# Lightning attention into an MLP: groups of one chunk of each sequence, and eight first MLP blocks on three chunks

## The chip, the cores and the metric

The kernel runs on one core of a Trainium2 chip. The core has five engines, each with its own instruction stream: TensorE (PE; its weight loads are listed as PEld), VectorE (DVE), ScalarE (ACT), GpSimd (POOL) and SyncE (SP). They run side by side and wait for each other through semaphores; transfers run on 16 DMA engines. The metric is the time of one execution on the device in microseconds, the median over runs; lower is better. Every instruction stream keeps the order in which the program emits it: the scheduling is manual, so the order of the Python calls is the order on each engine.

## The reference

Four sequences of 768 positions, eight heads of 64. Linear attention with a decay per head goes over a sequence in blocks, carrying a 64 x 64 state per head; its output is the input of an MLP with an exact GELU.

```python
for b in range(nb):
    intra = np.einsum('bhic,bhjc->bhij', qb, kb) * Dmask[None]
    intra = np.einsum('bhij,bhjd->bhid', intra, vb)
    inter = np.einsum('bhid,bhde->bhie', qb * lam_pow[None], kv_state)
    out[:, :, sl] = intra + inter
    kb_dec = kb * rev_pow[None]
    kv_state = lam_block[None, :, None, None] * kv_state + np.einsum('bhsd,bhse->bhde', kb_dec, vb)
x = out.transpose(0, 2, 1, 3).reshape(B * S, H * D)     # 3072 x 512
h = x @ w_in                                            # 512 -> 2048
g = 0.5 * h * (1.0 + erf(h / sqrt(2)))
return g @ w_out                                        # 2048 -> 512
```

Inputs and output are float32; matrix products take bfloat16 operands, into which the loads convert.

## The kernel before

The kernel uses chunks of 128 positions, so each of the four sequences has six, 24 in all. Chunk n is sequence n // 6, position n % 6: chunks 0 to 5 are the first sequence in order. Four consecutive chunks form a group, of 512 token rows, and the MLP runs on a group at a time; there are six groups.

A chunk passes through these steps. `load` (line 64) issues a transfer of q, k or v from GpSimd's queue. `decay_v` (146) multiplies v by a decay into `v_dec`, on VectorE for the first two chunks and on GpSimd for all others. `transposes` (151) turns k and q on TensorE, and ScalarE copies kT out while VectorE scales qT (chunks 0 to 7); chunks from 8 on are turned by DMA instead, issued from SyncE's queue (`dma_transposes`, 167). `scores` (173) multiplies kT and qT on TensorE, and VectorE masks the two halves into `sc_m`. `next_state` (184) multiplies k and `v_dec` on TensorE, and VectorE adds the previous state and scales the sum; it is left out for the last chunk of a sequence. `outputs` (227) multiplies state and qT (unless the chunk is the first of its sequence), adds `v_dec` times `sc_m`, and copies the sum into x, on ScalarE for chunks 0 to 7 and VectorE afterwards. State and output of the first four chunks use a special form with half-filled 64 x 64 matmuls (lines 189 to 210 and 233 to 238).

`mlp_blocks` (406) gives a group as a list of blocks. Sixteen `mm1` blocks multiply w_in with x, four matmuls of 512 columns each, and ScalarE applies GELU. Then group 0 has 16 `mm2` blocks of four matmuls of 512 columns against w_out. Groups 1 to 5 have 14 blocks that form the same product from seven half-sized products (`blocks_by_seven`, 275), with sums of g and of w_out made by VectorE between them (`g_sum`, `w_out_sum`); the products `m1` and `m7` share a bank `r`, and a VectorE step at line 386 (`f_x`) reads it between them.

The lead-in (lines 477 to 511) runs chunks 0 to 3 up to x, with idle matmuls (`keep_warm`) in between, before any MLP block. While the MLP of group g runs, the chunks of group g + 1 are prepared: for group 0 the dictionary `group0` (539) says which steps run ahead of which block; for later groups `todo` (552) places them by the share of matmul columns done. Loads go through GpSimd's queue in the order of the program, with `decay_v` in the same queue; a load also waits until the eighth transfer before it has landed (as its waits in the trace show). w_in comes in four pieces of 512 columns (512 KB each), the first after the loads of chunks 0 to 3, the fourth behind `decay_v` of chunk 3, then w_out in four.

Of the kernel before, what the change touches and what calls it, by code (L numbers as in the profile page):

```python
# [15 lines left out]
def kernel(  # L16
# [25 lines left out]
    assert NG * M == NCH and M == 4 and NB == 6  # L42
# [13 lines left out]

    raw = {}
    dram = dict(q=q, k=k, v=v)

    def chunk_of(name, n):  # L60
        b, so = n // NB, n % NB
        return dram[name][b, :, so * C:(so + 1) * C, :].rearrange("h si d -> si h d")
# [14 lines left out]
    for item in "k0 q0 v0 k1 q1 k2 q2 v1 k3 q3 v2 v3".split():  # L77
        load(int(item[1]), item[0])
# [7 lines left out]
    def load_w_in(s):  # L86
        f = d_ff // NS
        nc.gpsimd.dma_start(w_in_t[:, :, s * f:(s + 1) * f], w_in_r[:, :, s * f:(s + 1) * f])
# [16 lines left out]
    first_blk = consts.tile([128, HP, 128], BF16)  # L105
    nc.vector.memset(lam_blk, 0.0)
    nc.vector.memset(first_blk, 0.0)
# [32 lines left out]
    def begin(n, early=False):  # L140
        c = Chunk()
        c.n, c.sb, c.early = n, n % NB, early
        c.q, c.k, c.v = (raw.pop((n, name)) for name in "qkv")
        return c

    def decay_v(c, eng):

        c.v_dec = work_pool.tile([128, H, D], BF16, tag="vd", name="v_dec")
        eng.tensor_mul(c.v_dec, c.v, lam_m[:, :, None].to_broadcast((128, H, D)))  # L149

    def transposes(c, between=lambda: None):

        t_ps = [bank([128, HP, C], BF16, tag, "t_ps") for tag in ("mh", "mo" if c.early else "mh")]
        for dst, src in zip(t_ps, (c.k, c.q)):
            for hp in range(HP):
                nc.tensor.transpose(dst[:, hp, :], src[:, 2 * hp:2 * hp + 2, :], ident)  # L156
            if src is c.k:
                between()
        c.kT = work_pool.tile([128, HP, C], BF16, tag="kT", name="kT")
        c.qT = work_pool.tile([128, HP, C], BF16, tag="qT", name="qT")  # L160
        if c.n > 0:
# [22 lines left out]
    def next_state(c):  # L184
        if c.sb == NB - 1:
            return
        if not c.early:
            return next_state_full(c)
        kv_ps = bank([128, HP, D], F32, "t", "kv_ps")
        for hp in range(HP):  # L190
            for hi in range(2):
                h = 2 * hp + hi
                nc.tensor.matmul(kv_ps[hi * D:(hi + 1) * D, hp, :], c.k[:, h, :], c.v_dec[:, h, :],
                                 start=True, stop=True)
        if c.n == M - 1:
            tmp = work_pool.tile([128, HP, D], F32, tag="tmp", name="tmp")
            nc.vector.tensor_add(tmp, kv_ps, states[c.n][0])
            for hi in range(2):
                p = slice(hi * D, (hi + 1) * D)
                nc.vector.tensor_mul(first_blk[p, :, p], tmp[p], lam_c_b[p])  # L200
            states[c.n + 1] = first_blk, None
            return
        new = work_pool.tile([128, HP, D], BF16, tag="state", name="state")
        if c.sb == 0:
            nc.vector.tensor_mul(new, kv_ps, lam_c_b)
        else:
            tmp = work_pool.tile([128, HP, D], F32, tag="tmp", name="tmp")
            nc.vector.tensor_add(tmp, kv_ps, states[c.n][0])
            nc.vector.tensor_mul(new, tmp, lam_c_b)
        states[c.n + 1] = new, None  # L210

    def next_state_full(c):

        kv_ps = bank([128, HP, 128], F32, "t", "kv_ps")
        for hp in range(HP):
            nc.tensor.matmul(kv_ps[:, hp, :], c.k[:, 2 * hp:2 * hp + 2, :], c.v_dec[:, 2 * hp:2 * hp + 2, :],
                             start=True, stop=True)
        new = work_pool.tile([128, HP, 128], BF16, tag="state_f", name="state")
        if c.sb == 0:
            nc.vector.tensor_mul(new, kv_ps, lam_blk)  # L220
        else:
            tmp = work_pool.tile([128, HP, 128], F32, tag="tmp", name="tmp")
            nc.vector.tensor_add(tmp, kv_ps, states[c.n][0])
            nc.vector.tensor_mul(new, tmp, lam_blk)  # L224
        states[c.n + 1] = new, None

    def outputs(c, x_t, off, evacuate=True):
        o_ps = bank([128, HP, C], F32, "o", "o_ps")
        if c.sb > 0 and not c.early:
            for hp in range(HP):  # L230
                nc.tensor.matmul(o_ps[:, hp, :], states[c.n][0][:, hp, :], c.qT[:, hp, :],  # L231
                                 start=(hp == 0), stop=False, skip_group_check=True)
        elif c.sb > 0:
            for hp in range(HP):
                for hi in range(2):
                    p = slice(hi * D, (hi + 1) * D)
                    nc.tensor.matmul(o_ps[p, hp, :], states[c.n][0][p, hp, :], c.qT[p, hp, :],
                                     start=(hp == 0), stop=False, skip_group_check=True)
        for hp in range(HP):
            for hi in range(2):  # L240
                nc.tensor.matmul(o_ps[hi * D:(hi + 1) * D, hp, :], c.v_dec[:, 2 * hp + hi, :], c.sc_m[:, hp, hi, :],  # L241
                                 start=(c.sb == 0 and hp == 0), stop=True, skip_group_check=True)
# [32 lines left out]
    def blocks_by_seven(g, g_t, first):  # L275
# [47 lines left out]
        def store(rows, us, cols):  # L323
            r = g * M * C + rows * 2 * C
            dst = out[r + us.start * C:r + us.stop * C, cols].rearrange("(u p) d -> p u d", p=C)
            nc.sync.dma_start(dst, sb["o0" if rows == 0 else "o1"][:, us, cols])
# [78 lines left out]

    def mlp_blocks(g):
# [4 lines left out]
        def mm1(kf):  # L411
            def run():
                h_ps = bank([128, T], F32, "mh", "h_ps")

                parts = [(0, T - C), (T - C, T)] if g == 0 and kf == 0 else [(0, T)]
                for lo, hi in parts:
                    for ki in range(NK1):
                        nc.tensor.matmul(h_ps[:, lo:hi], w_in_t[:, ki, kf * 128:(kf + 1) * 128], x_t[:, ki, lo:hi],  # L418
                                         start=(ki == 0 and lo == 0), stop=(ki == NK1 - 1), skip_group_check=True)
                nc.scalar.activation(g_t[:, kf, :], h_ps, ACT.Gelu)  # L420
# [4 lines left out]
        def mm2(io, part):  # L425
            def run():
# [5 lines left out]
                if part == NK2 // 4 - 1:  # L432
                    o_sb = out_pool.tile([128, d_model], F32, tag="o_s", name="o_sb")
                    r = (g * M + io) * C
                    nc.scalar.copy(o_sb, om[io])
                    nc.sync.dma_start(out[r:r + C, :], o_sb)
# [3 lines left out]
        blocks = [(mm1(kf), 4 * T) for kf in range(NK2)]  # L440
        if g > 0:
            return blocks_by_seven(g, g_t, blocks)
# [58 lines left out]
    empty_outputs(live[1])
    next_state(live[2])
    outputs(live[2], xT[0], 2)
    scores(live[3])
    keep_warm(4)
    outputs(live[3], xT[0], 3)
    make_lam_blk()
    load_w_in(3)
# [8 lines left out]
    for n, name in [(4, "k"), (4, "q"), (4, "v"), (5, "k"), (5, "q"), (5, "v"), (6, "k"), (6, "q")]:  # L517
        load(n, name)
    begin_decayed(4)
    for n, name in [(6, "v"), (7, "k"), (7, "q"), (7, "v"), (8, "k")]:  # L520
        load(n, name)
    begin_decayed(5)
    begin_decayed(6)
    for n, name in [(8, "q"), (8, "v")]:
        load(n, name)
    begin_decayed(7)
    next_load[0] = 9
    prefetch(9)
# [5 lines left out]
    def place(at):  # L534
# [84 lines left out]
```

## Time and profile before

| | us |
|---|---|
| runs (3): median, lowest, highest | 214.67, 213.27, 215.45 |
| the profiled execution, device time | 213.38 |
| its span in the trace | 211.6 |
| first MLP matmul on TensorE | 19.64 |
| first mm2 matmul of group 0 | 33.82 |
| first MLP matmul of group 1 | 54.23 |

The profiled execution's device time is 1.8 us above its span; what lies around the span is taken as fixed. It is 1.3 us below the median of the runs. Times in the trace count from the span's start. The granted TensorE clock is full over the whole span. A line of a timeline gives start and length in us, engine, source line, operation, output and inputs, the number of instructions merged, and in brackets the idle time before with what ended it. The length of the last matmul in such a line runs past the start of the next, since matmuls are pipelined; costs are therefore taken from start to start.

### The profile page before, as it was taken

How to read it: one execution, taken by the hardware profiler on the slowest of the kernel's cores; microseconds unless marked ns; L12 is line 12 of the kernel's file. 1: busy time of each engine (PE TensorE's matmuls, PEld its weight loads, DVE VectorE, ACT ScalarE, POOL GpSimd, SP SyncE). 2: the span in 40 equal slices, each digit the busy share in tenths (PEclk: the TensorE clock that was granted, in tenths of full speed). 3: DMA queues.
4: the chain of work that ended last, by engine and by line, in shares of the span. 5: the costliest groups of instructions: out<-in, count | busy, mean ns of one | idle time of the engine just before them, and what ended most of it. 6: DMA issues, size and time to landing. Idle time of an engine off the chain costs nothing. (4 is left out here: it accounts for less than half of the span.)

```text
span 211.6 us, 4033 instructions
## 1 busy us (share of the span) xinstructions
PE 198.7 (94%) x1654; PEld 125.0 (59%) x1670; DVE 132.7 (63%) x219; ACT 79.9 (38%) x136; POOL 93.0 (44%) x108
## 2 busy tenths in 40 slices
PE   7778999999799999999999899999999999999992
PEld 2355444466345678644688545687545688544881
DVE  4696200287799999527799536589536799223382
ACT  6624663333565420265310265320265310366200
POOL 8978633599999646606336606342101000000000
PEclk9999999999999999999999999999999999999999
DMA  5999999999999999997995998990563000500014
GB/s 36 145 148 202 206 208 190 158 191 116 169 165 139 155 155 91 179 196 113 110 77 32 158 201 131 103 74 0 195 91 67 3 0 0 201 0 0 3 50 149
DMA packets 100258, 24.39 MB, mean 115 GB/s; under 512 B 92816, under 2 KB 97424, under 8 KB 100240
## 3 DMA queue, kind: packets, MB, share of 16 engines
q0 software_dynamic: 79104, 13.64, 85.2%
q1 hardware_dynamic: 21136, 10.50, 23.4%
q8 instruction: 13, 0.21, 0.4%
q14 instruction: 5, 0.04, 0.1%
HBM read 27.27 MB, written 6.29 MB: 159 GB/s over the span
## 5 line engine op out<-in xcount | busy, mean ns | idle before, releaser
L420 ACT ACTIVATE g_t<-h_ps 128x512 bf16<-128x512 f32 x96 | 57.3, 597 | 79.1 <-PE h_ps L418 79.1
L418 PE MATMUL h_ps<-x_t,w_in_t 128*128 128x512 bf16 (+2 forms) x377 | 84.6, 377 | 0.5
L418 PEld LDWEIGHTS <-w_in_t 128*128 128x128 bf16 x388 | 37.3, 98 | 42.8 <-issue 0.8
L149 POOL TENSOR_TENSOR v_dec<-v_t,lam_m 128x512 bf16<-128x512 bf16 x22 | 23.3, 1061 | 57.8 <-issue 36.6
L316 PEld LDWEIGHTS <-g_sum 128*128 128x128 bf16 x400 | 38.4, 98 | 7.7 <-DVE g_sum L289 1.6
L289 DVE TENSOR_TENSOR g_sum<-g_t 128x1024 bf16<-128x1024 bf16 x50 | 31.7, 683 | 10.7 <-ACT g_t L420 10.7
L182 DVE TENSOR_TENSOR sc_m<-sc_ps,cmask 128x512 bf16<-128x512 f32 x48 | 30.8, 682 | 10.0 <-PE sc_ps L178 9.8
L66 POOL DMA_DIRECT2D k_t<-in_k_dram x24 | 22.1, 919 | 3.9 <-DMA w_out_t<-in_moe_w_out_dram 2.1
L251 DVE TENSOR_TENSOR x_t<-o_ps,lam_q 128x512 bf16<-128x512 f32 x16 | 11.0, 685 | 20.4 <-PE o_ps L241 20.4
L66 POOL DMA_DIRECT2D q_t<-in_q_dram x24 | 21.6, 898 | 3.3 <-DMA w_out_t<-in_moe_w_out_dram 3.3
L66 POOL DMA_DIRECT2D v_t<-in_v_dram x24 | 21.4, 893 | 2.8 <-DMA w_out_t<-in_moe_w_out_dram 1.7
L316 PE MATMUL r_ps<-w_sum,g_sum 128*128 128x256 bf16 x160 | 19.1, 273 | 1.3 <-DVE f_x L386 1.3
L165 DVE TENSOR_TENSOR qT<-t_ps,lam_q 128x512 bf16<-128x512 bf16 x8 | 5.5, 689 | 19.1 <-PE t_ps L156 18.7
L316 PEld LDWEIGHTS <-g_t 128*128 128x128 bf16 x160 | 15.5, 98 | 2.8
L430 PE MATMUL o_ps<-w_out_t,g_t 128*128 128x512 bf16 x60 | 15.0, 380 | 0.3 <-issue 0.2
L178 PE MATMUL sc_ps<-qT,kT 64*128 64x128 bf16 x192 | 9.5, 218 | 1.9 <-DMA qT<-q_t 1.2
L224 DVE TENSOR_TENSOR state<-tmp,lam_blk 128x512 bf16<-128x512 f32 x13 | 10.6, 813 | 0.4
L316 PE MATMUL p_ps<-w_out_t,g_sum 128*128 128x256 bf16 x80 | 10.1, 273 | 0.7 <-DVE g_sum L289 0.7
L316 PE MATMUL p_ps<-w_sum,g_t 128*128 128x256 bf16 x80 | 10.2, 273 | 0.0
L241 PE MATMUL o_ps<-sc_m,v_dec 128*64 128x128 bf16 x192 | 10.0, 225 | 0.1
L162 ACT COPY kT<-t_ps 128x512 bf16<-128x512 bf16 x7 | 4.1, 586 | 14.9 <-PE t_ps L156 14.9
L316 PE MATMUL s_ps<-w_sum,g_sum 128*128 128x256 bf16 x80 | 9.6, 273 | 0.0
(69 smaller groups left out, 160.5 us busy)
## 6 DMA issues: line engine op xcount, KB each, us to landing
out_dram<-o_sb SPq DMA_DIRECT2D x9, 512.0 KB, 3.6
k_t<-in_k_dram POOLq DMA_DIRECT2D x24, 128.0 KB, 5.2
q_t<-in_q_dram POOLq DMA_DIRECT2D x24, 128.0 KB, 5.4
v_t<-in_v_dram POOLq DMA_DIRECT2D x24, 128.0 KB, 5.6
w_in_t<-in_moe_w_in_dram POOLq DMA_DIRECT2D x4, 512.0 KB, 8.9
w_out_t<-in_moe_w_out_dram POOLq DMA_DIRECT2D x4, 512.0 KB, 13.5
out_dram<-o_sb SPq DMA_DIRECT2D x5, 256.0 KB, 4.2
kT<-k_t SPq DMA_TRANSPOSE x16, 4.5
```

What stands on the lines that cost most here:

```text
L66: nc.gpsimd.dma_start(raw[n, name], chunk_of(name, n))
L149: eng.tensor_mul(c.v_dec, c.v, lam_m[:, :, None].to_broadcast((128, H, D)))
L178: nc.tensor.matmul(sc_ps[hi][:, hp, :], c.kT[p, hp, :], c.qT[p, hp, :], start=True, stop=True)
L182: nc.vector.tensor_mul(c.sc_m[:, :, hi, :], sc_ps[hi], mask)
L224: nc.vector.tensor_mul(new, tmp, lam_blk)
L241: nc.tensor.matmul(o_ps[hi * D:(hi + 1) * D, hp, :], c.v_dec[:, 2 * hp + hi, :], c.sc_m[:, hp, hi, :], start=(c.sb == 0 and hp == 0), stop ...
L251: nc.vector.tensor_mul(c.x_o, c.o_ps, lam_q)
L289: nc.vector.tensor_tensor(gsum[i][:, ks, :], g_t[:, ka + k:ka + k + n4, ta], g_t[:, kb + k:kb + k + n4, tb], op=op)
L316: nc.tensor.matmul(o, left[i](k, slice(u * C, (u + 1) * C)), right[i](k), start=(begin and k == 0), stop=(k == KH - 1), skip_group_check=True)
L418: nc.tensor.matmul(h_ps[:, lo:hi], w_in_t[:, ki, kf * 128:(kf + 1) * 128], x_t[:, ki, lo:hi], start=(ki == 0 and lo == 0), stop=(ki == NK1 ...
L420: nc.scalar.activation(g_t[:, kf, :], h_ps, ACT.Gelu)
L430: nc.tensor.matmul(om[io], g_t[:, kf, io * C:(io + 1) * C], w_out_t[:, kf, :], start=(kf == 0), stop=(kf == NK2 - 1))
```

## The change

Chunk n becomes sequence n % 4, position n // 4: a group holds the same position of all four sequences, the state of chunk n goes to chunk n + 4, and the rows of the output are addressed to match. Chunks 0 to 3 then start from no state, and the special form for the early chunks is removed with the state that they passed on. The buffers for `v_dec` and the state go from three to six.

The lead-in runs only chunks 0 to 2. w_in comes in eight pieces of 256 columns. The loads of chunk 3 are issued behind the first four of these and `decay_v` of chunk 2; its own `decay_v` behind the other four. The first eight `mm1` blocks run on the 384 columns of chunks 0 to 2. Chunk 3's transposes go ahead of block 7, and its scores, next_state and outputs ahead of block 8. Blocks 8 and 9 then do the 128 columns of chunk 3 for the same eight slices of w_in, four slices in one bank each, and eight full blocks follow, so there are 18 (`e`) `mm1` blocks. The steps of chunks 4 to 7 are placed one `mm2` block later in `group0`, and partly joined; the loads of chunks 4 to 9 and their `decay_v` are ordered anew.

```diff
+    out_r = out.rearrange("(b s p) d -> s p b d", b=M, p=C)
     def chunk_of(name, n):
-        b, so = n // NB, n % NB
+        so, b = n // M, n % M
-    for item in "k0 q0 v0 k1 q1 k2 q2 v1 k3 q3 v2 v3".split():
+    for item in "k0 q0 v0 k1 q1 v1 k2 q2 v2".split():
         load(int(item[1]), item[0])
-    def load_w_in(s):
-        f = d_ff // NS
-        nc.gpsimd.dma_start(w_in_t[:, :, s * f:(s + 1) * f], w_in_r[:, :, s * f:(s + 1) * f])
+    def load_w_in(kf, n):
+        f = slice(kf * 128, (kf + n) * 128)
+        nc.gpsimd.dma_start(w_in_t[:, :, f], w_in_r[:, :, f])
...
-        c.n, c.sb, c.early = n, n % NB, early
+        c.n, c.sb, c.early = n, n // M, early
-        c.v_dec = work_pool.tile([128, H, D], BF16, tag="vd", name="v_dec")
+        c.v_dec = work_pool.tile([128, H, D], BF16, tag="vd", name="v_dec", bufs=6)
-        t_ps = [bank([128, HP, C], BF16, tag, "t_ps") for tag in ("mh", "mo" if c.early else "mh")]
+        t_ps = [bank([128, HP, C], BF16, tag, "t_ps") for tag in ("mh mo" if c.n < M - 1 else "mo mo" if c.early else "mh mh").split()]
...
-        states[c.n + 1] = new, None
+        states[c.n + M] = new
...
-        if c.sb > 0 and not c.early:
+        if c.sb > 0:
             for hp in range(HP):
-                nc.tensor.matmul(o_ps[:, hp, :], states[c.n][0][:, hp, :], c.qT[:, hp, :],
+                nc.tensor.matmul(o_ps[:, hp, :], states[c.n][:, hp, :], c.qT[:, hp, :],
...
+    K3 = 8
-        def mm1(kf):
+        def mm1(kf, ks=1, cols=slice(0, T)):
+            n = cols.stop - cols.start
             def run():
-                h_ps = bank([128, T], F32, "mh", "h_ps")
-                parts = [(0, T - C), (T - C, T)] if g == 0 and kf == 0 else [(0, T)]
-                for lo, hi in parts:
+                h_ps = bank([128, ks, n], F32, "mh", "h_ps")
+                for k in range(ks):
                     for ki in range(NK1):
-                        nc.tensor.matmul(h_ps[:, lo:hi], w_in_t[:, ki, kf * 128:(kf + 1) * 128], x_t[:, ki, lo:hi],
-                                         start=(ki == 0 and lo == 0), stop=(ki == NK1 - 1), skip_group_check=True)
-                nc.scalar.activation(g_t[:, kf, :], h_ps, ACT.Gelu)
+                        nc.tensor.matmul(h_ps[:, k, :], w_in_t[:, ki, (kf + k) * 128:(kf + k + 1) * 128],
+                                         x_t[:, ki, cols], start=(k == 0 and ki == 0), stop=(ki == NK1 - 1),
+                                         skip_group_check=True)
+                nc.scalar.activation(g_t[:, kf:kf + ks, cols], h_ps, ACT.Gelu)
...
+        three, fourth = slice(0, T - C), slice(T - C, T)
+        blocks = [(mm1(kf, cols=three), 4 * 3 * C) for kf in range(K3)]
+        blocks += [(mm1(kf, 4, fourth), 4 * 4 * C) for kf in range(0, K3, 4)]
+        blocks += [(mm1(kf), 4 * T) for kf in range(K3, NK2)]
...
     early(1)
-    next_state(live[0])
-    outputs(live[0], xT[0], 0, evacuate=False)
+    outputs(live[0], xT[0], 0)
     scores(live[1])
     decay_v(live[1], nc.vector)
...
     keep_warm(1)
+    for kf in range(0, K3, 2):
+        load_w_in(kf, 2)
+    live[2] = begin(2, early=True)
     decay_v(live[2], nc.gpsimd)
+    transposes(live[2])
+    outputs(live[1], xT[0], 1)
+    keep_warm(1)
     scores(live[2])
+    keep_warm(4)
+    outputs(live[2], xT[0], 2)
+    make_lam_blk()
+    for name in "kqv":
+        load(3, name)
+    for kf in range(K3, NK2, 2):
+        load_w_in(kf, 2)
+    live[3] = begin(3, early=True)
     decay_v(live[3], nc.gpsimd)
...
+    for n in (4, 5, 6):
+        for name in "kqv":
+            load(n, name)
+    for n in (4, 5, 6, 7):
+        begin_decayed(n)
+        if n + 3 < 10:
+            for name in "kqv":
+                load(n + 3, name)
+    next_load[0] = 10
...
+    e = K3 + K3 // 4 + NK2 - K3
     group0 = {
-        1: [lambda: next_state(live[3])],
-        22: [lambda: transposes(live[4])],
-        24: [lambda: scores(live[4])],
-        25: [lambda: transposes(live[5]), lambda: next_state(live[4]), lambda: x1(4)],
-        26: [lambda: scores(live[5])],
-        27: [lambda: transposes(live[6])],
-        28: [lambda: x1(5), lambda: scores(live[6])],
-        29: [lambda: transposes(live[7]), lambda: next_state(live[6])],
-        30: [lambda: x1(6), lambda: scores(live[7])],
-        31: [lambda: next_state(live[7]), lambda: x1(7)],
+        2: [lambda: next_state(live[0])],
+        4: [lambda: next_state(live[1])],
+        6: [lambda: next_state(live[2])],
+        7: [lambda: transposes(live[3])],
+        8: [lambda: scores(live[3]), lambda: next_state(live[3]), lambda: outputs(live[3], xT[0], 3)],
+        e + 7: [lambda: transposes(live[4])],
+        e + 8: [lambda: scores(live[4]), lambda: next_state(live[4])],
+        e + 9: [lambda: x1(4)],
+        e + 10: [lambda: transposes(live[5])],
+        e + 11: [lambda: scores(live[5]), lambda: next_state(live[5])],
+        e + 12: [lambda: x1(5), lambda: transposes(live[6])],
+        e + 13: [lambda: scores(live[6]), lambda: next_state(live[6])],
+        e + 14: [lambda: x1(6), lambda: transposes(live[7])],
+        e + 15: [lambda: scores(live[7]), lambda: next_state(live[7]), lambda: x1(7)],
     }
```

Removed and not shown: `first_blk`, the half-filled forms of state and output, and the old lead-in.

More of the change, by code (lines that the diff above doesn't have):

```diff
@@ L41 @@
     NG = NCH // M
-    assert NG * M == NCH and M == 4 and NB == 6
+    assert NG * M == NCH and M == B == 4 and NG == NB == 6
     ctx.enter_context(tc.manual_schedule())
@@ L104 @@
     lam_blk = consts.tile([128, HP, 128], F32)
-    first_blk = consts.tile([128, HP, 128], BF16)
     nc.vector.memset(lam_blk, 0.0)
-    nc.vector.memset(first_blk, 0.0)
     ln = consts.tile([128, H], F32)
@@ L186, in next_state @@
             return
[L187 to L209, printed above, removed]
-        states[c.n + 1] = new, None
-    def next_state_full(c):
         kv_ps = bank([128, HP, 128], F32, "t", "kv_ps")
@@ L217, in next_state_full @@
                              start=True, stop=True)
-        new = work_pool.tile([128, HP, 128], BF16, tag="state_f", name="state")
+        new = work_pool.tile([128, HP, 128], BF16, tag="state_f", name="state", bufs=6)
         if c.sb == 0:
@@ L222, in next_state_full @@
             tmp = work_pool.tile([128, HP, 128], F32, tag="tmp", name="tmp")
-            nc.vector.tensor_add(tmp, kv_ps, states[c.n][0])
+            nc.vector.tensor_add(tmp, kv_ps, states[c.n])
             nc.vector.tensor_mul(new, tmp, lam_blk)
-        states[c.n + 1] = new, None
+        states[c.n + M] = new
     def outputs(c, x_t, off, evacuate=True):
         o_ps = bank([128, HP, C], F32, "o", "o_ps")
-        if c.sb > 0 and not c.early:
+        if c.sb > 0:
             for hp in range(HP):
-                nc.tensor.matmul(o_ps[:, hp, :], states[c.n][0][:, hp, :], c.qT[:, hp, :],
+                nc.tensor.matmul(o_ps[:, hp, :], states[c.n][:, hp, :], c.qT[:, hp, :],
                                  start=(hp == 0), stop=False, skip_group_check=True)
[L233 to L238, printed above, removed]
         for hp in range(HP):
@@ L323, in store @@
         def store(rows, us, cols):
-            r = g * M * C + rows * 2 * C
-            dst = out[r + us.start * C:r + us.stop * C, cols].rearrange("(u p) d -> p u d", p=C)
+            b = slice(rows * 2 + us.start, rows * 2 + us.stop)
+            dst = out_r[g, :, b, cols]
             nc.sync.dma_start(dst, sb["o0" if rows == 0 else "o1"][:, us, cols])
@@ L433, in run @@
                     o_sb = out_pool.tile([128, d_model], F32, tag="o_s", name="o_sb")
-                    r = (g * M + io) * C
                     nc.scalar.copy(o_sb, om[io])
-                    nc.sync.dma_start(out[r:r + C, :], o_sb)
+                    nc.sync.dma_start(out_r[g, :, io, :], o_sb)
             return run
         parts = NK2 // 4
-        blocks = [(mm1(kf), 4 * T) for kf in range(NK2)]
         if g > 0:
-            return blocks_by_seven(g, g_t, blocks)
+            return blocks_by_seven(g, g_t, [(mm1(kf), 4 * T) for kf in range(NK2)])
+        three, fourth = slice(0, T - C), slice(T - C, T)
+        blocks = [(mm1(kf, cols=three), 4 * 3 * C) for kf in range(K3)]
+        blocks += [(mm1(kf, 4, fourth), 4 * 4 * C) for kf in range(0, K3, 4)]
+        blocks += [(mm1(kf), 4 * T) for kf in range(K3, NK2)]
         blocks += [(mm2(io, part), 4 * 512) for pair in range(0, M, 2) for part in range(parts)
@@ L483 @@
     early(1)
-    next_state(live[0])
-    outputs(live[0], xT[0], 0, evacuate=False)
+    outputs(live[0], xT[0], 0)
     scores(live[1])
     decay_v(live[1], nc.vector)
-    load_w_in(0)
     keep_warm(1)
-    early(2)
-    load_w_in(1)
+    for kf in range(0, K3, 2):
+        load_w_in(kf, 2)
+    live[2] = begin(2, early=True)
     decay_v(live[2], nc.gpsimd)
-    load_w_in(2)
-    empty_outputs(live[0])
-    next_state(live[1])
+    transposes(live[2])
+    outputs(live[1], xT[0], 1)
+    keep_warm(1)
     scores(live[2])
-    outputs(live[1], xT[0], 1, evacuate=False)
-    keep_warm(1)
-    early(3)
-    decay_v(live[3], nc.gpsimd)
[L501 to L508, printed above, removed]
+    keep_warm(4)
[6 more added lines that the diff above has]
+    live[3] = begin(3, early=True)
+    decay_v(live[3], nc.gpsimd)
     for s in range(NS):
@@ L515, in begin_decayed @@
         decay_v(live[n], nc.gpsimd)
[L517 to L528, printed above, removed]
+    for n in (4, 5, 6):
[7 more added lines that the diff above has]
+    next_load[0] = 10
     total = NK2 * 4 * M * C + M * NK2 * 512
```

## The prediction

> **What bounds the kernel now.** I read the page's busy times first, then TensorE's waits over the whole run, then the timelines of the two stretches that the change rewrites.
>
> ```profile
> PE 198.7 (94%) x1654; PEld 125.0 (59%) x1670; DVE 132.7 (63%) x219; ACT 79.9 (38%) x136; POOL 93.0 (44%) x108
> ```
>
> TensorE is busy for 94% of the 211.6 us span, so a change must take away idle time or matmuls of that engine. The waits (total, times, longest, in us) say where idle time is left:
>
> ```profile
> PE kv_ps L193 <- DVE v_dec L149: 1.8, 2, 1.2
> PE r_ps L316 <- DVE f_x L386: 1.3, 2, 0.7
> ...
> PE sc_ps L178 <- DMA qT<-q_t: 1.2, 1, 1.2
> PE p_ps L316 <- DVE g_sum L289: 0.7, 3, 0.3
> ```
>
> The first is in the lead-in; the third is one wait at 57.27. The others are waits for VectorE late in a group. So there are 20 us of lead-in, 94% full work, and little else. The end of the lead-in on TensorE (start, length, line, tiles), then what VectorE and ScalarE do for the same chunk 3:
>
> ```profile
> 17.44 0.40 PE L178 MATMUL sc_ps<-qT,kT 64*128 64x128 bf16 x8
> 17.77 1.04 PE L471 MATMUL idle_ps<-idle 128*128 128x512 bf16 x3
> 18.74 0.41 PE L237 MATMUL o_ps<-qT,state 64*64 64x128 bf16 x8
> 19.08 0.52 PE L241 MATMUL o_ps<-sc_m,v_dec 128*64 128x128 bf16 x8
> 19.64 1.05 PE L418 MATMUL h_ps<-x_t,w_in_t 128*128 128x384 bf16 x8
> ```
>
> ```profile
> 17.87 1.29 DVE L182 TENSOR_TENSOR sc_m<-sc_ps,cmask 128x512 bf16<-128x512 f32 x2 [0.54 <-PE sc_ps L178]
> ```
>
> ```profile
> 19.63 0.59 ACT L249 CAST x_t<-o_ps 128x512 bf16<-128x512 f32 x1 [1.50 <-PE o_ps L241]
> ```
>
> Read across: from a chunk's scores (17.44) it takes 0.43 us to the masks, 1.29 for both, 0.44 more to the end of its outputs (19.60) and 0.62 to x (20.22): 2.8 us of latency with under 0.8 us of matmuls. Before, idle matmuls and the first block fill it. The join of groups 0 and 1:
>
> ```profile
> 51.26 0.40 PE L178 MATMUL sc_ps<-qT,kT 64*128 64x128 bf16 x8
> 51.59 1.04 PE L430 MATMUL o_ps<-w_out_t,g_t 128*128 128x512 bf16 x4
> 52.47 0.39 PE L216 MATMUL kv_ps<-v_dec,k_t 128*128 128x128 bf16 x4
> 52.69 0.39 PE L231 MATMUL o_ps<-qT,state 128*128 128x128 bf16 x4
> 53.01 0.41 PE L241 MATMUL o_ps<-sc_m,v_dec 128*64 128x128 bf16 x8
> 53.58 0.81 PE L430 MATMUL o_ps<-w_out_t,g_t 128*128 128x512 bf16 x3 [0.16 <-issue]
> 54.23 1.89 PE L418 MATMUL h_ps<-x_t,w_in_t 128*128 128x512 bf16 x8
> 57.27 0.40 PE L178 MATMUL sc_ps<-qT,kT 64*128 64x128 bf16 x8 [1.16 <-DMA qT<-q_t]
> ```
>
> Chunk 7's masks lie behind an MLP block (51.59), so its outputs do not wait. Group 1 starts at 54.23 and, two blocks on, loses 1.3 us (55.95 to 57.27) to chunk 8's transposed q.
>
> **Part 1, the lead-in: -2.8 us.** Chunks 0 to 2 become first chunks of three sequences: the state matmuls of lines 193 and 237 and the VectorE steps of 0.41 and 0.42 us go, and chunk 3 leaves. VectorE's chain still sets the pace: v_dec of chunk 1 at 12.63, qT of chunk 2 13.23 to 13.92, as before. Scores of chunk 2 then start at 13.97, masks run 14.4 to 15.7, outputs end 0.44 later at 16.15, x is copied by 16.8, and block 0 starts there instead of at 19.64. w_in must be there: POOL's v_dec of chunk 2, held by its v load, started at 14.68; that load moves from eleventh to ninth place, at 0.88 us per issue, to 12.9. In the old order v_dec of chunk 3 started at 17.08 behind its load and w_in's first 512 KB released TensorE at 19.6, 2.5 us on; so a 256 KB piece lands by 15.5 at the latest. Not on the path.
>
> **Part 2, the first MLP half: +4.0 us.** Its columns stay: 8 blocks of 4 x 384 at 0.162 us (starts of the 384-wide matmuls at 19.64) are 5.2 us, two of 16 x 128 at 0.056 are 1.8, and eight full ones at 0.863 are 6.9, together 13.9 against 13.8. Put in between: three more next_state (0.235 each), transposes 0.44, scores 0.33 and outputs 0.34 of chunk 3: 1.8 us that stood in the lead-in before. And waits: the transposes start at about 22.0, block 7 covers most of their evacuation (0.3 is left). But scores, next_state and outputs of chunk 3 and then the block that reads its x follow each other with nothing between. Of the 2.8 us of latency above, scores, next_state and outputs fill 0.9; the rest, 1.9, is bare. So 2.2 us of waits, between 1.5 (evacuation already done) and 3 (a late q or v load of chunk 3). For those loads: 128 KB loads follow each other by 0.85 us and 512 KB of weights by 2.53 (POOL's issues of v, k, q at 24.82, 27.33, 29.87 are each released by such a piece), which is 0.29 us fixed and 0.56 per 128 KB, so 1.4 for a 256 KB piece: four land by 19.7, k, q and v of chunk 3 by 20.6, 21.4 and 22.3, and v_dec (1.04 on POOL, which has only issues ahead of it) by 23.4, against needs at 22.0 and 23.75. Just in time. The half ends at 16.8 + 18.0 = 34.9; before, 33.8.
>
> **Part 3, the second half of group 0: +1.6 us.** Everything of chunks 4 to 7 moves one block later, but the last slot now holds scores, next_state and outputs of chunk 7 together. From scores the outputs end after 0.43 + 1.29 + 0.42 = 2.14 us where their matmuls need 1.2: 0.9 us bare. Chunks 4 to 6 have one block between, 0.05 to 0.17 us bare each: 0.2. Chunk 5 gets a next_state (0.235) and chunk 6 state matmuls (0.32), for neither is the last or the first of its sequence now. On POOL the order is decay, three loads, decay: 1.04 + 2.7 per chunk, so v_dec of chunk 7 is ready 3 x 3.75 us after that of chunk 4 (42.4), at 53.65, needed at 53.8. Group 1 starts near 57.0 instead of 54.23.
>
> **Part 4, the wait at 57.27: -1.3 us.** A group that starts 2.8 us later finds qT of chunk 8 landed, if that slips little. k of chunk 8 is issued at about 46.15 (before 44.87), q at 47.05 (before 47.80): I take a slip of 0 to 1 us, below the 1.45 that are left. Less than 0 would gain nothing, as TensorE is then the later one.
>
> **Part 5, groups 1 to 4: +1.0 us.** State matmuls for chunks 12 and 18 add 0.64; next_state from chunk 8 on runs 12 times instead of 13: -0.24. The waits for VectorE move. Group 1 has no next_state for its last chunk (11) now, group 2 has (15), and there line 316 waits:
>
> ```profile
> 84.70 0.41 PE L241 MATMUL o_ps<-sc_m,v_dec 128*64 128x128 bf16 x8
> 85.05 1.92 PE L316 MATMUL r_ps<-w_sum,g_sum 128*128 128x256 bf16 x16
> ...
> 115.97 0.41 PE L241 MATMUL o_ps<-sc_m,v_dec 128*64 128x128 bf16 x8
> 116.91 1.91 PE L316 MATMUL r_ps<-w_sum,g_sum 128*128 128x256 bf16 x16 [0.53 <-DVE f_x L386]
> ```
>
> The two VectorE steps (0.7 each) ahead of f_x are the difference. With chunk 11 taking part, group 1 waits 0.53 to 0.8 (VectorE runs without a gap there): +0.6. The mid-group wait of 0.2 appears in group 3 and goes from group 4. Six v_dec buffers instead of three free POOL at 72.91, where TensorE does not wait; the row stride of stores and loads changes no size: 0.
>
> **Sum.** -2.8 + 4.0 + 1.6 - 1.3 + 1.0 = +2.5 us, on the profiled execution 213.38 + 2.5 = 215.9. That one lies 1.3 under the median of the runs, 214.67, so I forecast 217.1.
>
> **A rule against the change.** By the rows a piece costs 0.29 us beyond its bytes, so four more pieces delay w_out and chunks 4 to 7 by 0 (if the bytes alone count) to 1.2 us. [...]
>
> **Rivals.** (a) The transfers decide. w_out's last piece lands at 37.6 now (issued at 21.17, 16.4 us to landing); 42.4 for v_dec of chunk 4 already has 1.2 us for the pieces in it. When weights followed loads in the old order, the loads that POOL's v_dec at 14.68 and 17.08 waited for landed 2.4 us apart instead of 0.85; the new order has that switch twice. Another 1.5 us makes 43.9, and next_state of chunk 4 wants it at 42.6: +1.3, and up to +2.3 if the join is late as well, so 218.4 to 219.4. For it: DMA moves data without a pause from 6 to 48 us. Against: w_out itself has slack (its last piece is needed at 40.1). 0.15. (b) Faster: the bare waits of parts 2 and 3 (3.3) are covered, group 1 starts at 53.7, and chunk 8's q, issued 0.75 earlier, brings its scores to 56.5. With part 5's matmuls (+0.4) that ends 0.35 before the old time, 214.3; as states come from four chunks back, VectorE's old waits (2.0) might go too, 212.3. It decides if TensorE idles under 0.3 us between the scores of chunk 3 and the first 128-wide block. Against it stand the masks' 1.29 us and the copy's 0.59. 0.08. (c) About half of the waits: chunk 3's latency is as predicted, but VectorE keeps ahead in group 1 and the slot of chunk 7 overlaps better: +0.7 to +1.9, 215.4 to 216.6. 0.30. (d) The change does not start its blocks early, because w_in comes after 16.8: all behind it shifts along, bounded as (a). 0.03.
>
> **How the numbers follow.** The forecast (216.6 to 218.2) has 0.44, (a) and (d) 0.18, (b) 0.08, (c) 0.30. A difference under 1%, 2.15 us, is about what a measurement here cannot tell from no change, and the forecast's sum is close above it. Slower by over 1% holds (a), (d) and nearly all of the forecast, 0.58; within 1% hold (c), the rest of the forecast and a part of (b), 0.36; faster by over 1%, 0.06. The range 214.3 to 219.3 leaves out most of (b) and the far end of (a).
>
> **What would show it.** Block 0 at 16.8 on TensorE; two gaps of over 0.5 us there between 23 and 27; the first line 430 matmul near 34.9; outputs of chunk 7 about 0.9 us behind its state matmuls; no wait for qT near 58; a wait for f_x in group 1. If block 8 follows the scores of chunk 3 without a gap, or a wait for w_out_t or v_dec near 40 to 44 is the longest, the sum is wrong.

## The result and the profile after

The changed kernel takes 222.97 us (median of 4, 220.74 to 224.0), the kernel before, on the same chip, 215.06 (median of 4, 213.27 to 218.94). The ratio is 1.038, 95% interval 1.026 to 1.050: slower by some 8 us, where 2.5 were forecast. Measured again on a chip where the kernel before took 216.91, it took 222.44: 1.030 (1.016 to 1.045). Medians are over all executions, while ratios leave out those in a second, slower state, so a ratio can differ from the quotient of the medians. The profiled execution took 222.79, 9.4 more than that of before. Where it lies, from the timelines of TensorE (us from the span's start; "three buffers" is experiment e1, "again" a second profile of the changed kernel, e12):

| | before | after | again | three buffers |
|---|---|---|---|---|
| first MLP matmul | 19.64 | 16.91 | 16.95 | 17.05 |
| first mm2 matmul of group 0 | 33.82 | 36.62 | 35.06 | 35.17 |
| first MLP matmul of group 1 | 54.23 | 58.78 | 58.01 | 58.24 |
| first MLP matmul of group 2 | 86.80 | 96.50 | 96.73 | 91.08 |
| end of span | 211.6 | 221.0 | 221.3 | 216.1 |

Two stretches differ most from the forecast: the first half of group 0 in one profile of the two, and group 1, which takes 37.7 and 38.7 us instead of 32.6. From group 2 to the end nothing is lost. The page of the changed kernel gives the engines' busy times and, in 40 slices, the granted clock:

```profile
PE 203.6 (92%) x1670; PEld 129.5 (59%) x1670; DVE 138.5 (63%) x217; ACT 80.1 (36%) x138; POOL 96.5 (44%) x112
...
PEclk9999889999999996999999999999999999999999
```

TensorE's share falls by 2 points, so idle time grew. VectorE has two instructions fewer but 5.8 us more busy time. Some of that is other work, as the half-width state steps of the early chunks gave way to full ones: in e10 and e9, where none of its steps is lengthened, the old order keeps it busy for 130.4 us and the new one for 132.4. By these, lengthened steps cost it 2.3 us before and 6.1 after. And the clock, full over the whole span before (0.998 on average), is below full in slices 5, 6 and 16 (0.984 on average). TensorE's waits, longest totals first:

```profile
PE p_ps L282 <- DVE g_sum L255: 4.8, 3, 4.4
PE o_ps L207 <- DVE sc_m L181: 1.6, 5, 0.4
PE r_ps L282 <- DVE f_x L352: 1.5, 3, 0.5
PE h_ps L386 <- ACT x_t L215: 1.3, 2, 0.7
```

The second and the fourth are the bare waits that the prediction counted, but for 0.23 and 0.67 us of them in the lead-in. The two gaps ahead of chunk 3's outputs matmuls are these; the third, of 0.67 us for its x, follows at 26.34:

```profile
24.68 0.22 PE L207 MATMUL o_ps<-sc_m,v_dec 128*64 128x128 bf16 x1 [0.43 <-DVE sc_m L181]
25.28 0.38 PE L207 MATMUL o_ps<-sc_m,v_dec 128*64 128x128 bf16 x7 [0.38 <-DVE sc_m L181]
```

The wait for qT of chunk 8 is gone, as it said. The first line is new: one wait of 4.4 us for a g_sum in group 1. Around it, TensorE's timeline and VectorE's:

```profile
79.20 0.60 PE L282 MATMUL p_ps<-w_out_t,g_sum 128*128 128x256 bf16 x4
84.16 2.61 PE L282 MATMUL p_ps<-w_out_t,g_sum 128*128 128x256 bf16 x12 [4.36 <-DVE g_sum L255]
```

```profile
64.95 7.43 DVE L236 TENSOR_TENSOR w_sum<-w_out_t 128x1024 bf16<-128x1024 bf16 x8
...
74.81 1.28 DVE L196 TENSOR_TENSOR state<-tmp,lam_blk 128x512 bf16<-128x512 f32 x1
76.02 4.36 DVE L255 TENSOR_TENSOR g_sum<-g_t 128x1024 bf16<-128x1024 bf16 x5
```

In the kernel before the same eight and five steps, one merged line each, took:

```profile
61.17 5.74 DVE L270 TENSOR_TENSOR w_sum<-w_out_t 128x1024 bf16<-128x1024 bf16 x8
...
69.95 3.09 DVE L289 TENSOR_TENSOR g_sum<-g_t 128x1024 bf16<-128x1024 bf16 x5
```

Eight undisturbed w_sum steps take 4.9 us (in e9), so VectorE lost 2.5 us here and 1.3 in g_sum. GpSimd's decays in the same time (the lines of `v_dec` alone), in the kernel before and after it:

```profile
63.28 1.27 POOL L149 TENSOR_TENSOR v_dec<-v_t,lam_m 128x512 bf16<-128x512 bf16 x1
67.51 1.04 POOL L149 TENSOR_TENSOR v_dec<-v_t,lam_m 128x512 bf16<-128x512 bf16 x1 [0.32 <-DMA v_t<-in_v_dram]
72.91 1.04 POOL L149 TENSOR_TENSOR v_dec<-v_t,lam_m 128x512 bf16<-128x512 bf16 x1 [1.72 <-PE o_ps L241]
80.76 1.04 POOL L149 TENSOR_TENSOR v_dec<-v_t,lam_m 128x512 bf16<-128x512 bf16 x1 [4.19 <-issue]
```

```profile
62.55 1.06 POOL L148 TENSOR_TENSOR v_dec<-v_t,lam_m 128x512 bf16<-128x512 bf16 x1
66.23 1.50 POOL L148 TENSOR_TENSOR v_dec<-v_t,lam_m 128x512 bf16<-128x512 bf16 x1
70.37 1.46 POOL L148 TENSOR_TENSOR v_dec<-v_t,lam_m 128x512 bf16<-128x512 bf16 x1
74.47 1.06 POOL L148 TENSOR_TENSOR v_dec<-v_t,lam_m 128x512 bf16<-128x512 bf16 x1
78.15 1.06 POOL L148 TENSOR_TENSOR v_dec<-v_t,lam_m 128x512 bf16<-128x512 bf16 x1
```

With three buffers GpSimd stops at 71 until an outputs step frees a `v_dec`, and at 77 again, for 4.19 us, where the profile names no releaser (in e1 an outputs step ends both such stops). With six it goes on, and five decays instead of four start between 62 and 81 us, none of them held back. VectorE has six long steps there (1.3 to 2.0 us instead of 0.68). Five overlap a decay, one of these by 0.06 us only; the sixth, a w_sum from 68.81 to 70.33, ends just ahead of one.

The clock shows in the windows (stretch, its length, then busy time and instructions of PE, PEld, DVE, ACT, POOL; granted clock, DMA share, GB/s):

```profile
22.00:26.00 4.00, 2.71 (x34) 1.87 (x33) 2.95 (x5) 1.76 (x4) 4.00 (x6) 1.00 1.44 197
26.00:30.00 4.00, 3.66 (x34) 3.54 (x34) 0.00 (x0) 0.96 (x3) 3.44 (x5) 0.57 1.25 207
...
80.00:84.00 4.00, 0.00 (x0) 0.00 (x0) 3.97 (x7) 0.00 (x0) 3.99 (x6) 1.00 2.28 155
84.00:88.00 4.00, 3.84 (x20) 2.81 (x21) 2.43 (x5) 0.00 (x0) 1.51 (x2) 0.57 2.13 137
```

After chunk 3's gaps and after the wait for g_sum the clock averages 0.57 over 4 us. In windows of 0.4 us it stands at 0.50 from 26.4 to 29.6 and from 84.4 to 87.6, and at 1.00 before and after but for the one window on either side: half speed for 3.4 us each time. Ahead of the second, no matmul ran from 80 to 84. Ahead of the first TensorE was not idle: it was busy for 2.71 of the 4 us before 26 (more on this in the last section). What makes the clock fall and come back, and when, no run shows.

### The profile page after: what moved, and what is told of

Its sections match the earlier page's. It is cut to its first block, busy times and chain, and to the rows that moved or that the text cites. A ratio compares the mean times of both kernels' runs of the same rounds, so it can differ in the third digit from the quotient of the medians.

```text
span 221.0 us, 4053 instructions
## 1 busy us (share of the span) xinstructions
PE 203.6 (92%) x1670; PEld 129.5 (59%) x1670; DVE 138.5 (63%) x217; ACT 80.1 (36%) x138; POOL 96.5 (44%) x112
## 3 DMA queue, kind: packets, MB, share of 16 engines
q1 hardware_dynamic: 21136, 10.50, 20.4%
## 5 line engine op out<-in xcount | busy, mean ns | idle before, releaser
L389 ACT ACTIVATE g_t<-h_ps 128x512 bf16<-128x512 f32 (+1 forms) x98 | 57.7, 588 | 87.3 <-PE h_ps L386 87.2
L386 PE MATMUL h_ps<-x_t,w_in_t 128*128 128x512 bf16 (+2 forms) x416 | 88.0, 370 | 1.3 <-ACT x_t L215 1.3
L386 PEld LDWEIGHTS <-w_in_t 128*128 128x128 bf16 x416 | 40.4, 102 | 42.0 <-issue 2.1
L282 PEld LDWEIGHTS <-g_sum 128*128 128x128 bf16 x400 | 39.4, 100 | 12.5 <-DVE g_sum L255 5.6
L148 POOL TENSOR_TENSOR v_dec<-v_t,lam_m 128x512 bf16<-128x512 bf16 x22 | 23.9, 1089 | 38.2 <-PE o_ps L207 29.7
L255 DVE TENSOR_TENSOR g_sum<-g_t 128x1024 bf16<-128x1024 bf16 x50 | 33.0, 710 | 10.7 <-ACT g_t L389 10.7
L164 DVE TENSOR_TENSOR qT<-t_ps,lam_q 128x512 bf16<-128x512 bf16 x8 | 5.5, 688 | 19.7 <-PE t_ps L155 19.7
L282 PE MATMUL p_ps<-w_out_t,g_sum 128*128 128x256 bf16 x80 | 11.2, 292 | 4.8 <-DVE g_sum L255 4.8
L196 DVE TENSOR_TENSOR state<-tmp,lam_blk 128x512 bf16<-128x512 f32 x16 | 14.1, 882 | 0.6
L195 DVE TENSOR_TENSOR tmp<-kv_ps,state 128x512 f32<-128x512 f32 x16 | 10.9, 680 | 0.0
L282 PE MATMUL q_ps<-w_out_t,g_sum 128*128 128x256 bf16 x80 | 10.1, 283 | 0.0
```

What stands on the lines that cost most here:

```text
L255: nc.vector.tensor_tensor(gsum[i][:, ks, :], g_t[:, ka + k:ka + k + n4, ta], g_t[:, kb + k:kb + k + n4, tb], op=op)
L282: nc.tensor.matmul(o, left[i](k, slice(u * C, (u + 1) * C)), right[i](k), start=(begin and k == 0), stop=(k == KH - 1), skip_group_check=True)
L386: nc.tensor.matmul(h_ps[:, k, :], w_in_t[:, ki, (kf + k) * 128:(kf + k + 1) * 128], x_t[:, ki, cols], start=(k == 0 and ki == 0), stop=(ki ...
L389: nc.scalar.activation(g_t[:, kf:kf + ks, cols], h_ps, ACT.Gelu)
```

## The experiments

All ratios are to the kernel before, run beside it on the same chip, with 95% intervals. The theories: **A**, the six buffers let GpSimd run on, which stretches VectorE in group 1; **C**, the clock halves after chunk 3's gaps; **E**, VectorE's load in group 1 is what turns the stretching into time; **G**, the stretching comes from GpSimd's decays.

**e1: three v_dec buffers.**

```diff
-        c.v_dec = work_pool.tile([128, H, D], BF16, tag="vd", name="v_dec", bufs=6)
+        c.v_dec = work_pool.tile([128, H, D], BF16, tag="vd", name="v_dec", bufs=3)
```

> The changed kernel with three v_dec buffers again instead of six; nothing else differs. Theory A (six buffers let GpSimd run its decays and load issues through the middle of group 1, where they stretch VectorE's steps; TensorE then waits 4.4 us for a g_sum and loses half its clock for 3.4 us): GpSimd waits for a buffer between 70 and 85, VectorE's w_sum and g_sum steps there go back to 0.68 us but for one or two, the wait for g_sum falls from 4.36 to under 1 us, the half clock near 84 is gone, and the time falls by 4.5 to 6 us, to 217 to 218.5. Rival B (VectorE is late in group 1 because the group starts later and has a next_state more; the buffers do not matter): the wait stays above 3 us and the time within 1 us of the changed kernel.

Measured 218.87 us, ratio 1.0125 (1.007 to 1.018). GpSimd's decays of this kernel, and all that is left of the wait for g_sum:

```profile
63.22 1.06 POOL L148 TENSOR_TENSOR v_dec<-v_t,lam_m 128x512 bf16<-128x512 bf16 x1
68.41 1.54 POOL L148 TENSOR_TENSOR v_dec<-v_t,lam_m 128x512 bf16<-128x512 bf16 x1 [1.52 <-PE o_ps L207]
76.53 1.04 POOL L148 TENSOR_TENSOR v_dec<-v_t,lam_m 128x512 bf16<-128x512 bf16 x1 [3.94 <-PE o_ps L207]
```

```profile
PE p_ps L282 <- DVE g_sum L255: 0.6, 3, 0.2
```

VectorE's eight w_sum steps and five g_sum steps, which took 7.43 and 4.36 us, are shorter again:

```profile
63.03 6.03 DVE L236 TENSOR_TENSOR w_sum<-w_out_t 128x1024 bf16<-128x1024 bf16 x8
...
72.09 3.09 DVE L255 TENSOR_TENSOR g_sum<-g_t 128x1024 bf16<-128x1024 bf16 x5
```

The buffer count alone is worth 3.6 to 4.1 us (against the 222.44 and 222.97 of the changed kernel, which did not run beside it), a little less than A expected. Side by side on one chip, e3 and e4 below, which also differ in the buffer count alone, are 3.8 apart. The wait and both half clocks are gone (mean granted clock 0.998), and group 1 takes 32.8 us. B falls. What remains over the kernel before is 3.5 us by the medians and 2.7 by the ratio; the prediction had forecast 2.5 for the whole change.

**e2: six buffers in the kernel before.** The same edit the other way round.

> The kernel before with six v_dec buffers instead of three; nothing else differs. Theory A: GpSimd no longer waits for buffers at 72 and from 76 to 81, more of VectorE's steps between 60 and 80 take 1.3 us or more (three did), TensorE's wait for g_sum in group 1 grows from 0.34 to 2 us or more, and the time rises by 2 to 5 us. Rival B: no change, within 0.5 us.

Measured 221.21 us, ratio 1.022 (1.014 to 1.030): slower by 5.8 us by the medians and 4.7 by the ratio. A had said 2 to 5. The place is not as A said: group 1 loses nothing to g_sum. TensorE's timeline, and GpSimd's ahead of it:

```profile
101.08 0.40 PE L178 MATMUL sc_ps<-qT,kT 64*128 64x128 bf16 x8 [3.67 <-DMA qT<-q_t]
```

```profile
87.22 0.89 POOL L66 DMA_DIRECT2D q_t<-in_q_dram  x1
88.11 0.88 POOL L66 DMA_DIRECT2D v_t<-in_v_dram  x1
89.00 1.06 POOL L149 TENSOR_TENSOR v_dec<-v_t,lam_m 128x512 bf16<-128x512 bf16 x1
89.99 0.92 POOL L66 DMA_DIRECT2D k_t<-in_k_dram  x1
```

Unhindered, GpSimd puts load after load (79 to 96 us without a pause) beside SyncE's transposes, and qT of chunk 13 comes 3.7 us late, with a half clock behind the wait: the 24 MLP matmuls from 101.81 on take 6.67 us, where 24 take 5.2 at the full clock (0.863 for four). That the loads delay it is read from this one profile. If so, the three buffers throttled GpSimd in two respects, and which one costs depends on the order around it.

**e3: the gaps of chunk 3 filled.**

```diff
-        8: [lambda: scores(live[3]), lambda: next_state(live[3]), lambda: outputs(live[3], xT[0], 3)],
+        8: [lambda: scores(live[3]), lambda: next_state(live[3]), lambda: keep_warm(5),
+            lambda: outputs(live[3], xT[0], 3), lambda: keep_warm(3, new=False)],
```

> The changed kernel with idle matmuls in chunk 3's two gaps: five of 512 columns ahead of its outputs and three behind them. Theory C (the bare waits of chunk 3 make TensorE's clock halve from 26.3 to 29.7, which doubles the 128-wide blocks 8 and 9): the granted clock stays 1.0 there, blocks 8 and 9 take 1.8 us together instead of 3.4, the first mm2 matmul comes near 35.0 instead of 36.6, and group 1 starts 1.6 us earlier; the g_sum wait of group 1 stays, so the time falls by 1.2 to 2 us. Rival D (the 128-wide blocks are slow because each matmul loads weights for 128 columns only, not because of the clock): they stay at 0.107 us a matmul and the time does not fall.

Measured 222.48 us, ratio 1.027 (1.018 to 1.036): no gain that can be told. The clock stayed full at 26, and mm2 started at 35.09 as C said, but group 1 still at 58.47, and the wait for g_sum was 4.3 us again. Behind that wait the clock averages 0.57 from 82 to 90 us, so the half clock lasts twice as long as the 3.4 us in the first profile of the changed kernel (there 0.57 over 4 us), which takes back part of what was gained at 26. That this is not a general gain has a second reason: the half clock at 26 does not come in every execution. The first line is from the changed kernel's first profile, the second from its second:

```profile
26.34 10.45 PE L386 MATMUL h_ps<-x_t,w_in_t 128*128 128x128 bf16 x64 [0.67 <-ACT x_t L215]
```

```profile
26.37 8.85 PE L386 MATMUL h_ps<-x_t,w_in_t 128*128 128x128 bf16 x63 [0.67 <-ACT x_t L215]
```

The same matmuls behind the same gaps take 1.6 us more or not. e1, which has the gaps too, kept the full clock. D falls: the 128-wide matmuls are slow with the clock alone (the 32 of blocks 8 and 9 take 3.36 us in the first profile, at a clock of 0.50; in the second the row leaves 1.8 for them beside eight full blocks at 0.863).

**e4: three buffers and filled gaps.** Both edits.

> Three v_dec buffers and the idle matmuls together. If theories A and C both hold and are separate, the two gains add: 6 to 7.5 us below the changed kernel, 215.5 to 217, which is the forecast of the prediction (its sum had neither). If the clock or the contention is only moved to another place, less than 5 us are gained.

Measured 218.69 us, ratio 1.017 (1.012 to 1.022): the same as e1. The gains do not add; what came is the second case, less than 5 us (4.3 below the 222.97). The profile has mm2 at 34.77 and group 1 at 57.0, but a wait of 2.57 us for g_sum, with a g_sum of 1.53 us and a w_sum of 1.99: three buffers make the collisions fewer, they don't exclude them, and what TensorE gains in group 0 it can lose to VectorE in group 1.

**e5 and e6: w_sum in group 0**, with six and with three buffers.

```diff
-    w_sums_left = [(i, half) for i in W_SUMS for half in range(2)]
+    w_sums_left = [(i, half) for half in range(2) for i in W_SUMS]
...
-                if g == 1 and i < 10:
-                    w_out_sum(*w_sums_left.pop(0))
...
+        e + 1: [lambda: [w_out_sum(*s) for s in w_sums_left]],
```

> The changed kernel, still with six v_dec buffers, with VectorE's ten w_sum steps moved from the MLP blocks of group 1 into group 0, behind its first mm2 block, where VectorE idles from 26 to 43 us. Theory E (VectorE sets the end of group 1's first half: with six buffers GpSimd's steps stretch it by 5 us there, and the 6 to 7 us of w_sum are what leaves it no room): the wait for g_sum falls from 4.4 to under 1 us although the buffers stay six, the half clock near 84 is gone, and the time falls by 4 to 6 us below the changed kernel. Rival F (GpSimd's early loads delay the transposed k and q or the stores, and VectorE is a bystander): the wait goes over to a DMA and the time stays within 1.5 us.

> Three v_dec buffers and the w_sum steps in group 0. Theory E: against three buffers alone (218.9) only the residual VectorE waits of group 1 go, 0 to 1.5 us; about 217.5 to 218.9. Rival F: no difference from three buffers alone.

Measured 221.41 us, ratio 1.023 (1.013 to 1.033), and 220.13, 1.018 (1.007 to 1.029). Neither is told apart from the kernel that it was made from. In e5, whose profile is of its longest execution (223.12 us), the wait for g_sum fell to 1.0 us, but TensorE then waited for VectorE elsewhere:

```profile
PE r_ps L280 <- DVE f_x L350: 3.6, 3, 2.5
PE sc_ps L177 <- DVE qT L164: 2.8, 5, 1.6
PE o_ps L207 <- DVE sc_m L181: 1.5, 5, 0.4
PE p_ps L280 <- DVE g_sum L255: 1.4, 3, 1.0
```

E holds for one wait; the 4 to 6 us that it forecast did not come (1.0 to 1.6 by the medians, with intervals that overlap). VectorE still has steps of 1.5 to 2.2 us beside GpSimd's decays, without w_sum. In e6 the sums themselves stand in front of chunk 4's qT (TensorE waited 1.55 us for it), which had been named as a risk only for the kernel before.

**e7: the bare places covered**, on top of e6.

```diff
-        6: [lambda: next_state(live[2])],
-        7: [lambda: transposes(live[3])],
-        8: [lambda: scores(live[3]), lambda: next_state(live[3]), lambda: outputs(live[3], xT[0], 3)],
+        6: [lambda: next_state(live[2]), lambda: transposes(live[3])],
+        7: [lambda: scores(live[3])],
+        8: [lambda: next_state(live[3]), lambda: keep_warm(2), lambda: outputs(live[3], xT[0], 3),
+            lambda: keep_warm(3, new=False)],
...
-        e + 13: [lambda: scores(live[6]), lambda: next_state(live[6])],
-        e + 14: [lambda: x1(6), lambda: transposes(live[7])],
-        e + 15: [lambda: scores(live[7]), lambda: next_state(live[7]), lambda: x1(7)],
+        e + 13: [lambda: scores(live[6]), lambda: transposes(live[7])],
+        e + 14: [lambda: x1(6), lambda: scores(live[7]), lambda: next_state(live[6])],
+        e + 15: [lambda: x1(7), lambda: next_state(live[7])],
```

> As the one before, and the two bare places covered: chunk 3's transposes one block earlier and its scores ahead of block 7, with idle matmuls in what is left of the gaps; in the last slots of group 0 chunk 7's transposes and scores one block earlier and the two next_state behind them. By the prediction's terms the first saves 0.6 us and the second 0.9, and a half clock at 26 cannot come: 1.5 us below the one before, 216 to 217.4. If qT of chunk 8 lands no earlier than in the changed kernel (58.0), half of it is lost there: 0.5 to 0.8.

Measured 218.16 us, ratio 1.016 (1.007 to 1.024). It misses the 216 to 217.4 expected. The median is 2 us below e6's, but the intervals overlap, and the ratio isn't below e1's 1.0125. Inconclusive for the sizes of parts 2 and 3.

**e8: the kernel before with w_sum in group 0.**

> The kernel before with the w_sum steps in group 0, ahead of block 17. Theory E says that VectorE has little to spare in group 1 of the kernel before too: TensorE's waits for g_sum and f_x in group 1 (0.34 and less) go, and executions in which GpSimd collides more often are helped more: 0.3 to 1.5 us faster. If VectorE is then late for chunk 4's qT (w_out's last piece lands at 37.6, its five sums take 3 us, qT of chunk 4 is due at 39.8), up to 1 us is lost instead.

Measured 215.24 us, ratio 1.002 (0.998 to 1.007): no change, where 0.3 to 1.5 us were expected. TensorE's waits for VectorE in group 1 were down to 0.2 us, from 0.3, so there was little to gain in the old order.

**e9: v_dec on ScalarE** for chunks 4 to 23, six buffers.

```diff
+    def decay_v_act(c):
+        c.v_dec = work_pool.tile([128, H, D], BF16, tag="vd", name="v_dec", bufs=6)
+        for h in range(H):
+            nc.scalar.activation(c.v_dec[:, h, :], c.v[:, h, :], ACT.Copy, scale=lam_m[:, h:h + 1])
...
     def begin_decayed(n):
         live[n] = begin(n)
-        decay_v(live[n], nc.gpsimd)
...
```

`decay_v_act` stands behind the transposes of each chunk.

> The changed kernel, six buffers, with v_dec of chunks 4 to 23 made by ScalarE in eight steps a chunk instead of by one step on GpSimd; GpSimd only issues transfers then. Theory G (what stretches VectorE is that it shares a path with GpSimd: its steps with two operands in SBUF, state, w_sum and g_sum, run at the same time as GpSimd's decay steps or its transfer issues): with the decays gone, at most two of VectorE's steps between 40 and 90 us take over 1 us instead of six, the wait for g_sum in group 1 is under 1 us, and the time is 3 to 6 us below the changed kernel in the same call. If transfer issues alone stretch VectorE as much, four or more such steps stay. Rival H (the six buffers cost time through the transfers that GpSimd issues earlier, whoever makes v_dec): waits for qT from DMA appear and the time stays within 1.5 us of the changed kernel.

Measured 226.25 us, ratio 1.053 (1.040 to 1.066): slower, where G had forecast 3 to 6 us less than the changed kernel. The time went to waits for ScalarE (below), but the run isolates the collision. VectorE between 55 and 95 us, grouped by form (busy us, mean ns), first of the changed kernel, then of this one:

```profile
L236 DVE TENSOR_TENSOR w_sum<-w_out_t 128x1024 bf16<-128x1024 bf16 x10 | 8.7, 932 | 0.0
L255 DVE TENSOR_TENSOR g_sum<-g_t 128x1024 bf16<-128x1024 bf16 x10 | 7.6, 809 | 0.0
L196 DVE TENSOR_TENSOR state<-tmp,lam_blk 128x512 bf16<-128x512 f32 x6 | 7.2, 1198 | 0.2
L195 DVE TENSOR_TENSOR tmp<-kv_ps,state 128x512 f32<-128x512 f32 x5 | 3.4, 678 | 0.0
```

```profile
L260 DVE TENSOR_TENSOR g_sum<-g_t 128x1024 bf16<-128x1024 bf16 x10 | 6.3, 684 | 0.0
L241 DVE TENSOR_TENSOR w_sum<-w_out_t 128x1024 bf16<-128x1024 bf16 x10 | 6.2, 685 | 0.0
L201 DVE TENSOR_TENSOR state<-tmp,lam_blk 128x512 bf16<-128x512 f32 x6 | 4.2, 692 | 0.2
```

With decays on GpSimd the three steps whose operands both lie in SBUF average 932, 809 and 1198 ns; without, all stand at 684 to 692, no VectorE step of the whole run takes over 1 us, and TensorE waits for a g_sum for 0.2 us at most, although GpSimd still issues the same transfers and the buffers are six. `tmp`, which reads one operand from PSUM, never stretched (at most 682 ns over the whole run of the changed kernel, 684 on average here). So it is the decays that lengthen the steps, as theory G has it, and H falls. That the two engines share a path was the author's guess; which steps are lengthened the rows show, by what path no trace does. What the time was lost to instead is in TensorE's waits of this kernel:

```profile
PE h_ps L391 <- ACT g_t L394: 6.0, 5, 1.3
PE kv_ps L193 <- ACT v_dec L153: 2.8, 11, 0.3
```

Eight steps of ScalarE stand ahead of a GELU in its queue, 2 us at a time.

**e10 and e11: ScalarE's decays** in the kernel before (chunks 8 to 23, three buffers) and on top of e7 (six buffers).

> The kernel before with v_dec of chunks 8 to 23 made by ScalarE, three buffers as before. Theory G: the two or three stretched VectorE steps of group 1 go and the spread between executions gets smaller; 0 to 2 us faster. If ScalarE's eight steps stand ahead of a GELU that TensorE waits for, or GpSimd, freed of its waits, issues loads so early that chunk 13's qT is late as in the six-buffer run, up to 4 us slower.

> All covers of the bare places (chunk 3, chunk 7, w_sum in group 0) and ScalarE's decays, six buffers. If theory G and the prediction's terms are the whole of it, the new order runs without its waits: 1 to 2 us above the kernel before, 215.5 to 217, and never below it, because its first half of group 0 still holds chunk 3's matmuls and qT of chunk 8 lands at 57 to 58.

Measured 222.66 us, ratio 1.035 (1.020 to 1.049), and 226.95, 1.053 (1.042 to 1.064). Both miss: no VectorE step over 1 us in either, and four or five waits of TensorE for a GELU at up to 1.3 us each, and one of 2.5 for x. ScalarE is no free engine where a GELU is due every 0.86 us.

**e12: the changed kernel again.**

> The changed kernel once more, so that its time stands on the same chip beside the others, and for a second profile: 220.5 to 224.5. [...]

222.44 us; its profile is the column "again". The wait for g_sum was 2.5 us, where the first profile had 4.4, and another of 2.9 for f_x, two stops of the same VectorE backlog; group 1 took a microsecond longer than in the first profile. No half clock at 26, one at 93 (mean granted clock 0.988).

No version was faster than the kernel before.

## Why the prediction was wrong, point by point

- **Part 1, -2.8:** -2.7 (block 0 at 16.91 instead of 19.64). Right; w_in was in time.
- **Part 2, +4.0:** from block 0 to mm2 18.1 us in e1 and e12 against 14.2, so +3.9: right, with the two gaps where they were put. In the first profile it was 19.7, as the clock halved. The prediction had the granted clock of before, full throughout, and did not ask what a stretch in which matmuls stream for a third of the time would do to it: a missing term of 1.6 us, in some executions.
- **Part 3, +1.6:** 22.2 us against 20.4 in the first profile, +1.75: right. In e1 and e12 it was +2.7 and +2.5, each with a wait of 0.9 to 1.0 for a qT behind a state step of 1.5 to 1.6 us: VectorE was stretched here too. A mis-sized term, up to 1 us, for the same reason as the next.
- **Part 4, -1.3:** right; scores of chunk 8 start at 60.60 with no wait, against 58.7 forecast, as the group starts later. In e1 0.76 us of it comes back as a wait for qT of chunk 9.
- **Part 5, +1.0:** this is the step that failed, in its last clause: "Six v_dec buffers instead of three free POOL at 72.91, where TensorE does not wait ...: 0." TensorE did not wait there because GpSimd was waiting; the longer stop of 4.19 us before 80.76 was not looked at. Freed, GpSimd ran its decays against VectorE's sums. VectorE ended its fifth g_sum 21.6 us after the start of group 1, against 16.9 in e1; TensorE stopped for 4.4 us, and the clock halved behind the stop. Worth 3.6 to 4.1 us by e1. Of the part's other terms, the wait for f_x in group 1 was 0.41 (0.53 in e1), for 0.53 to 0.8; the matmuls added and dropped were not measured apart. In e1 all that follows the start of group 1 takes 0.5 us more than before, where parts 4 and 5 give 0.3 less.
- **Rivals:** none came. (a) is refuted by the waits: in the changed kernel's two profiles and in e1's TensorE waited for no w_out_t and, near 40 to 44, for no v_dec. The fixed cost of a transfer, 0.29 us by the prediction's rows, did no harm either; w_out's last piece landed 0.9 us earlier than before in the first profile, and 0.7 and 1.1 later in e1 and e12, within the 0 to 1.2 worked out.
- **The forecast of 217.1** fits e1 (218.87 beside a 215.41 of before) better than the change: the order was priced to within 2 us (2.7 by the ratio, 4.5 between the profiles, for 2.5), the buffers not at all. That the change came out slower, as forecast, owes about half or more of its 8 us to terms that the sum did not have.

Not settled: how the 3.5 us of e1 divide between chunk 3's gaps, the last slot of group 0 and collisions that remain; e4, e6 and e7 differ by less than their intervals. That what e2 lost comes from DMA queues is read from one profile.

## What to carry to other kernels

A buffer count is also a throttle: before raising it, look at what the engine that waits for a buffer would do with the time, in which queue and beside which steps of other engines. An engine's wait "that costs nothing" is costed by laying the work that it would release over the other engines' timelines, here GpSimd's decays over VectorE's steps with two SBUF operands (684 to 692 ns on average without the decays, 809 to 1198 with them). Where a change opens gaps on TensorE, allow for a half clock behind them: here it came behind chunk 3's gaps in some executions only, for 3.4 us, and once, behind a wait, for twice that.

## What the runs showed of the hardware that was not expected

One collision of a GpSimd decay (1.04 us) with a VectorE step of 0.68 us made that step mostly 1.3 to 1.6 us long and now and then 1.8 to 2.35, and the decay up to 1.5. Not every long step has a decay beside it: in e12 a w_sum from 58.62 to 60.15 took 1.53 us beside load issues alone. Issues alone lengthened nothing in e9, so what happened there stays open. The half clock came behind stretches that were not empty: matmuls streamed for about 1.2 of the last 3.4 us before 26.3, a stretch as long as the half clock itself (block 7's rest, scores, next_state and outputs, from their starts in the timeline); in the profiles of e1, e5 and e12 the same code kept its clock.
